# One attention and feed-forward kernel on one core: three written-out orders replaced, and the state's last products cut from 16 to 12 steps

## The chip, the cores and the metric

The kernel runs on one core of a Trainium2 chip. Its time is the device time of one execution in microseconds. The profile shows one execution; its span starts with the first instruction and ends with the last.

## The reference

`x` has the shape 8 x 8 x 512 x 64 (batch, head, row, depth) and `state` 8 x 8 x 32 x 64. All inputs and the output are float32.

```python
scores = scale * x @ state.T            # 512 x 32 for each batch and head
a = softmax(scores);   xread = a @ state
scores2 = scale * state @ x.T           # 32 x 512
a2 = softmax(scores2); sread = a2 @ x
y = concat([xread, sread], axis=rows)   # 544 rows for each batch, 8 heads x 64 = 512 columns
xn = (y - mean) / sqrt(var + 1e-6) * g_ln
out = y + relu(xn @ w_ch1) @ w_ch2      # 512 -> 2048 -> 512
```

Each softmax subtracts the row's maximum and divides by the sum plus 1e-9. The output is 8 x 544 x 512.

## The kernel before, in words

Every float32 factor of a large product is scaled by a power of two and split into two float16 parts, a high one (`hi`) and what is left (`lo`). A product of two split factors is taken in three float16 terms (`TERMS`: hi hi, hi lo, lo hi). The TensorE (PE) does the products; the ScalarE (ACT) writes high parts and exponentials, the VectorE (DVE) low parts, reductions and small arithmetic, the GpSimd (POOL) a few element-wise steps; the SyncE (SP) issues nearly all transfers.

The 512 rows of a batch go through the first layer in a shortened way. Since `xread = a @ state`, `state_products(b)` multiplies the state by the first weights once (a `matrix` for each of four units u of 512 hidden columns), and `first_products(b)` multiplies the softmax numerators (`ea`) by it. `hidden` applies the relu and splits the result; `second_products(b)` multiplies by the second weights. For batch 0, `second_products_by_units` does this unit by unit as the weights become ready. `attention(b)` does the rest of a batch: loads (`x_f`, `s_j`, `s_r`), scaling, transposes by DMA (`sT`, `xT`, `ebT`), scores, both softmaxes, the read of the state (`read_state`, L396, then `fold_halves`, L409, and `sread`), copies of the numerators (`ek`), and the product `mix` (L432), which gives the rows to be normalised and added at the end. The 256 rows of the state's reads of all batches are kept in DRAM (`sread_rows`) and go through both layers at the very end: `state_rows`, `state_hidden` (L657) and `second_products(B)`.

The weights arrive as 64-bit words of which two 32-bit halves are put together. `weights1(u)` loads them (`raw`), rebuilds float32 numbers in `words` (`w1_t`), takes out the column means (L516), finds the largest column sum (L525) for the scale, splits, and copies four pieces of 256 KB into `w1c[u]`, in which the high and low parts of a head lie on different partition halves. `weights2(u)` does the like for the second weights.

Each of these functions is a generator that yields its instructions one at a time. `issue` gets a list of such streams and a written-out order: letter a is the first stream, b the second, and the number is the place within the stream. Each engine carries out its own instructions in this order; an instruction that waits holds back all behind it on its engine. Transfers issued by SP are in SP's order in the same way. At the seam of two orders an engine's first steps of the second can stand before last steps of the first: the trace shows loads and a reduction of the next batch there.

There are three orders. PLAN is the prologue: a `gain`, b `attention(0)`, c to f `weights1(0..3)`, g `state_products(0)`, h `first_products(0)`, i to l `weights2(0..3)`, m `attention(1)`, n `state_products(1)`, o `second_products_by_units`, p `common_scale`, q `first_products(1)`, r `second_products(1)`, s `attention(2)`, t `state_products(2)`. BATCH is used four times (b = 2 to 5): a `first_products(b)`, b `second_products(b)`, c `attention(b+1)`, d `state_products(b+1)`. LAST holds batches 6 and 7 and the state's rows.

Places that matter below, by number:

- in `weights1` (c, d, e, f): 0 and 1 load; 2 to 7 rebuild words; 8 the means on PE; 9 to 12 their subtraction on DVE; 13 sizes on ACT; 14 their sum on PE (L525); 15 to 18 the scale on DVE; 19 the high half on ACT; 20 the low half on DVE; 21 and 22 copies of the high half, 23 and 24 of the low half. The copies read `raws[1]`, and `weights2` writes its `w2_t` into buffers that served so: that of i is the one from which c21 to c24 read, that of j the one from which f21 to f24 read;
- in `attention` (b, m, s, or c in BATCH): 0 and 1 load `x_f`; 2 `s_j`; 3 to 6 `s_r`; 11 the reduction over `s_j` on DVE; 23, 28, 33 the transposes of `sT` and `xT`; 34 and 35 the split of `s_r`; 36 and 37 the scores; 38 to 40, 49 to 55 and 60 the first softmax; 41 to 45 the second softmax with the transpose `ebT` (45); 56 `read_state`; 57, 58 the fold; 59 `sread`; 63 to 71 the copies to `ek`; 72 to 75 the stores of `sread`; 77 and 79 the two halves of `mix`. For batch 0 the numbers differ: 14, 15, 18, 20 and 32 are low parts and reductions on DVE, 40 is `ebT`, 58 and 59 `read_state` and the copy after it;
- in `state_products` (g, d in BATCH): 0, 3, ..., 21 the products, two for a unit.

In the PSUM, `accumulator` gives five buffers in turn and `banks` one pair, used by the scores, the read of the state and both halves of `mix` one after the other. `rows`, `quad` and `halves` are pairs of buffers, used in turn.

Of the kernel before, what the change touches and what calls it, by code (L numbers as in the profile page):

```python
# [9 lines left out]
F16 = mybir.dt.float16  # L10
# [16 lines left out]
SN = 4.0  # L27
# [37 lines left out]
BATCH = (  # L65
# [7 lines left out]
LAST = (  # L73
# [698 lines left out]
```

## Time and profile before

| | before |
|---|---|
| median of 3 runs | 707.6 us (705.15 to 709.07) |
| the profiled execution | 707.91 us |
| its span | 706.1 us |
| mean granted clock of PE | 0.974 |
| PE busy | 655.7 us (93%) |
| DVE busy | 370.9 us (53%) |
| ACT busy | 365.3 us (52%) |
| POOL busy | 68.0 us (10%) |

Where the profile gives slices, each is a fortieth of the span and each digit the busy tenths. Nearly all instructions carry L110, the line of the helper that records them, so they are told apart by the names of what they write and read ("out<-in"). In a list in order of time, the columns are start (us), duration (us; of the whole group where "x" is over 1), engine, line, operation, shape, count, and in brackets how long the engine had been idle before and what ended it. SPq is SP's queue of transfers: its durations are those of issuing, not of landing. The chain is the sequence of work that ended last, followed back to the start.

### The profile page before, as it was taken

To read this page: it belongs to the slowest core of one execution; us is meant where nothing else is said; L and a number is where in the kernel's file an instruction comes from. 1 tells how busy PE (TensorE), PEld (TensorE's weight loads), DVE (VectorE), ACT (ScalarE), POOL (GpSimd) and SP (SyncE) were. 2 spreads that over 40 slices of the span, in tenths; PEclk is the share of its full clock that TensorE was granted. 3 is DMA by queue.
4 is the path that set the end of the run, shared out by engine and by line. 5 is a ranking of instruction groups with operands and counts; after the bars stand their busy time and mean duration, and the time that the engine had idled before them with its cause. 6 is when DMAs were issued, how large, how long until landed. Compare 5 with 4: busy or idle time off the path is not lost.

```text
span 706.1 us, 10278 instructions
## 1 busy us (share of the span) xinstructions
PE 655.7 (93%) x4129; PEld 320.8 (45%) x4132; DVE 370.9 (53%) x670; ACT 365.3 (52%) x588; POOL 68.0 (10%) x54
## 2 busy tenths in 40 slices
PE   1565989999999999899999999999999999999997
PEld 0232645444453444444444444444444345445763
DVE  5995889655624454354635462545365834421120
ACT  5585889986413933295419541773287545410220
POOL 0000463211200002000200020002000200000000
PEclk9867899999999999999999999999999999999999
DMA  8988794636251032503070306130524060140001
GB/s 325 326 217 197 232 209 119 123 74 135 59 138 61 8 60 55 148 30 68 16 185 32 68 8 162 63 64 8 124 90 68 1 135 5 59 61 1 31 31 30
DMA packets 97392, 67.52 MB, mean 96 GB/s; under 512 B 73600, under 2 KB 89472, under 8 KB 96896
## 3 DMA queue, kind: packets, MB, share of 16 engines
q1 hardware_dynamic: 95424, 63.19, 35.1%
q0 software_dynamic: 864, 3.15, 2.5%
q8 instruction: 32, 0.52, 0.3%
q10 hardware_dynamic: 1056, 0.53, 0.3%
q14 instruction: 16, 0.13, 0.1%
HBM read 28.05 MB, written 9.44 MB: 53 GB/s over the span
## 4 chain that ended last, share of the span: by engine, by line
PE 70%; DVE 9%; DMA 8%; SPq 5%; ACT 4%; POOL 2%; issue 1%; POOLq 0%; DVEq 0%; ACTq 0%
PE acc L673 37%; PE acc L616 20%; SPq L110 5%; PE acc L657 4%; PE acc L582 3%; DMA w1c<-raw 2%; POOL ts L110 2%; DVE w_t L110 2%; PE acc L516 2%; DMA s_j<-in_state_dram 1%; DMA s_r<-in_state_dram 1%; PE banks L432 1%; DMA raw<-in_moe_w_ch_dram 1%; DVE raw L110 1%; DMA ebT<-eb 1%
## 5 line engine op out<-in xcount | busy, mean ns | idle before, releaser
L673 PE MATMUL acc<-w2h,hid 128*128 128x512 f16 x1632 | 368.2, 382 | 0.0
L673 PEld LDWEIGHTS <-hid 128*128 128x128 f16 x1632 | 158.2, 99 | 192.7 <-issue 12.6
L616 PE MATMUL acc<-ea,matrix 128*128 128x512 f16 (+1 forms) x864 | 176.1, 356 | 1.0 <-DVE matrix L110 0.7
L616 PEld LDWEIGHTS <-matrix 128*128 128x128 f16 x864 | 82.6, 98 | 84.6 <-issue 5.5
L110 DVE TENSOR_TENSOR hid<-strip,hid 128x512 f16<-128x512 f32 x120 | 81.2, 697 | 71.4 <-ACT hid L110 71.1
L110 ACT ACTIVATE strip<-acc,hs 128x512 f32<-128x512 f32 x112 | 75.5, 681 | 53.5 <-PE acc L616 29.6
L110 ACT ACTIVATE hid<-strip 128x512 f16<-128x512 f32 x136 | 83.0, 626 | 7.6 <-PE acc L673 4.9
L110 ACT ACTIVATE matrix<-acc 128x512 f16<-128x512 f32 x64 | 36.2, 602 | 64.1 <-PE acc L582 64.1
L110 DVE SCALAR_TENSOR_TENSOR xr<-acc,of_second,xr 128x512 f32<-128x512 f32 x28 | 21.0, 748 | 64.7 <-PE acc L673 64.6
L110 DVE SCALAR_TENSOR_TENSOR matrix<-acc,matrix 128x512 f16<-128x512 f32 x64 | 41.8, 680 | 20.8 <-ACT matrix L110 20.7
L582 PE MATMUL acc<-w1c,sT 128*32 128x512 f16 x512 | 38.2, 397 | 10.7 <-DMA w1c<-raw 10.3
L110 POOL TENSOR_TENSOR ts<-ts,mA 128x1024 f32<-128x1024 f32 (+1 forms) x8 | 16.1, 2016 | 232.8 <-DVE mA L110 202.6
L110 ACT ACTIVATE strip<-acc,hr 128x512 f32<-128x512 f32 x8 | 5.4, 686 | 49.4 <-PE acc L657 49.4
L110 POOL TENSOR_TENSOR rs<-rs,mhalf 128x4 f32<-128x4 f32 (+1 forms) x10 | 9.5, 955 | 199.6 <-DVE rs L110 199.6
L657 PE MATMUL acc<-xsT,w1c 128*128 128x256 f16 x256 | 28.4, 273 | 0.0
L110 POOL TENSOR_TENSOR hid<-strip,hid 128x512 f16<-128x512 f32 x16 | 22.1, 1405 | 58.7 <-ACT hid L110 58.6
L110 DVE SCALAR_TENSOR_TENSOR x<-x_f,x_s,x 128x512 f16<-128x512 f32 x32 | 25.3, 804 | 4.4 <-ACT x L110 4.3
L657 PEld LDWEIGHTS <-w1c 128*128 128x128 f16 x256 | 25.1, 98 | 3.5
L110 ACT ACTIVATE xr<-banks,ux 128x1024 f32<-128x1024 f32 x14 | 15.7, 1119 | 20.2 <-PE banks L432 20.2
L110 ACT ACTIVATE ea<-ef 128x1024 f16<-128x1024 f32 (+1 forms) x9 | 8.5, 958 | 33.5 <-DVE ef L110 33.5
L110 DVE BATCH_NORM_STATS2 s<-xr 128x6 f32<-128x512 f32 x32 | 21.4, 686 | 8.1 <-ACT xr L110 7.5
L582 PEld LDWEIGHTS <-sT 128*32 128x32 f16 x512 | 10.4, 97 | 30.5 <-issue 24.0
(112 smaller groups left out, 514.4 us busy)
## 6 DMA issues: line engine op xcount, KB each, us to landing
raw<-in_moe_w_ch_dram SPq DMA_DIRECT2D x16, 1024.0 KB, 8.2
out_dram<-xr SPq DMA_DIRECT2D x16, 512.0 KB, 2.7
x_f<-in_x_dram SPq DMA_DIRECT2D x15, 512.0 KB, 5.9
w1c<-raw SPq DMA_DIRECT2D x16, 256.0 KB, 6.9
ek<-ea SPq DMA_DIRECT2D x56, 64.0 KB, 2.1
ek<-ek SPq DMA_DIRECT2D x7, 512.0 KB, 4.4
xr<-part POOLq DMA_DIRECT2D x6, 512.0 KB, 5.3
s_r<-in_state_dram SPq DMA_DIRECT2D x28, 64.0 KB, 4.1
```

The costliest lines, as they stand in the source:

```text
L110: return lambda: f(*map(now, args), **{k: now(v) for k, v in kw.items()})
L432: nc.tensor.matmul(px[:, c, D * h:D * h + D], lhsT=ek[:, h // 4, h % 4, (2 * t + c) * P:(2 * t + c + 1) * P], rhs=sk[:, h], start=True, st ...
L516: nc.tensor.matmul(ps, lhsT=gm[:, k:k + 1].broadcast_to([P, P]), rhs=t4[:, k], start=k == 0, stop=k == 3)
L582: nc.tensor.matmul(ps[32 * j:32 * j + 32], lhsT=sT[:, g, a, 32 * j:32 * j + 32], rhs=w[:, 2 * g + j // 2, j % 2], start=a == 0, stop=a == ...
L616: nc.tensor.matmul(o, lhsT=m[:, g, i, P * q:P * q + P], rhs=ea[:, s, k, g], start=g == 0 and n == 0 and (b > 0 or q % 2 == 0), stop=g == 1 ...
L657: nc.tensor.matmul(ps[:, 256 * f:256 * f + 256].rearrange("p (t n) -> p t n", t=2), lhsT=w[:, k // 2, k % 2, P * (q + f):P * (q + f) + P], ...
L673: nc.tensor.matmul(po, lhsT=hid[:, i, q, c * P:(c + 1) * P], rhs=w[:, j, q], start=first and q == 0 and n == 0, stop=last and q == 3 and n ...
```

## The change

The three orders PLAN, BATCH and LAST are replaced by others. In PLAN the streams are the same; the copies of weight halves, the loads and the steps that depend on them stand elsewhere. In BATCH the load of `s_j` (c2) comes first, two loads of `s_r` come after the transpose of `sT`, and `ebT` (c45) stands ahead of the copies to `ek`. LAST gets a further stream, `high_halves`: eight copies that bring the high halves of `w1c` together, two heads on the 128 partitions, in buffers that held raw weights before. With them `state_hidden` no longer doubles the low parts of the state's rows: it has 8 steps for high parts against `w1c` and 4 for low parts against the high halves alone, where it had 8 and 8; one product, low by low, is left out. The last eight stores go out from SP and ACT in turn.

The code:

```diff
+    high = [None] * U
+
+    def high_halves():
+
+        for t in range(2):
+            pair = extra(t, "high").bitcast(F16).rearrange("p (u k f) -> p u k f", u=2, k=4)
+            for u in (2 * t, 2 * t + 1):
+                high[u] = pair[:, u % 2]
+                for s in range(2):
+                    half = slice(64 * s, 64 * s + 64)
+                    yield do(nc.sync.dma_start, out=high[u][half], in_=w1c[u][half, :, s])
...
-            v = xn.rearrange("p (h d) -> p h d", h=H).unsqueeze(2).broadcast_to([P, H, 2, D])
-            pc = halves("pc").rearrange("p (a h i d) -> p a h i d", a=2, h=H, i=2)
-            yield do(nc.scalar.activation, pc[:, 0], v, AF.Copy, scale=SN)
-            for i in range(2):
-                yield do(nc.vector.scalar_tensor_tensor, pc[:, 1, :, i], xn.rearrange("p (h d) -> p h d", h=H), SN,
-                         pc[:, 0, :, i], ALU.mult, ALU.subtract)
...
+            v = xn.rearrange("p (h d) -> p h d", h=H)
+            pc = halves("pc")[:, 0:12 * P]
+            hi = pc[:, 0:8 * P].rearrange("p (h i d) -> p h i d", h=H, i=2)
+            lo = pc[:, 8 * P:12 * P].rearrange("p (h d) -> p h d", h=H)
+            yield do(nc.scalar.activation, hi, v.unsqueeze(2).broadcast_to([P, H, 2, D]), AF.Copy, scale=SN)
+            yield do(nc.vector.scalar_tensor_tensor, lo, v, SN, hi[:, :, 0], ALU.mult, ALU.subtract)
+            yield do(nc.sync.dma_start_transpose, out=xsT[:, t], in_=pc)
...
-        def multiply(ps, q, w, xsT):
+        def multiply(ps, q, w, wn, xsT):
             for f in range(2):
-                for k in range(H):
-                    for a in range(2):
...
+                fs = slice(P * (q + f), P * (q + f) + P)
+                for k in range(12):
+                    nc.tensor.matmul(ps[:, 256 * f:256 * f + 256].rearrange("p (t n) -> p t n", t=2),
+                                     lhsT=w[:, k // 2, k % 2, fs] if k < H else wn[:, k - H, fs], rhs=xsT[:, :, k],
+                                     start=f == 0 and k == 0, stop=k == 11, skip_group_check=True)
...
     def store_state(t):
         for j in range(4):
-            yield do(nc.sync.dma_start, out=out[4 * t + j, S:S + NS, :], in_=results[B][0][1][t][32 * j:32 * j + 32, 0])
+            yield do((nc.sync, nc.scalar)[j % 2].dma_start, out=out[4 * t + j, S:S + NS, :],
+                     in_=results[B][0][1][t][32 * j:32 * j + 32, 0])
```

The orders, cut to the lines spoken of here:

```diff
 PLAN = (
-    "b1 b3-4 b2 b0 b5 a0 b6-11 b22 b72 b12 d0 d3 b23-25 b13 b15 b14 b17-18 d2 d4 d1 d6 b19-20 d5 d7 e1 e5-6 e0 "
...
-    "m9 b59 b74 c19 c21 e20 f8 e23-24 m8 b92 m7 m10 b80 b60 c20 c22-23 i5 g6-7 f11 b90-91 m12-13 f12 g9 b93 "
-    "g10 c24 f9 m14-15 f10 f13 i3 e21 g0 g15 g1 m16 b41 m17 g11 m18 m20 f14 m31 g8 m29 g3 m24 i4 f15 i6 g4 f16 "
...
+    "b3 b0 d0 b1 b4 b2 b5-6 a0 b7-11 b22 b12 b72 b24 b13 b19 b17 d3 b23 d2 b25 b14 b20 b18 d1 d5-6 d4 d7 e1 "
...
+    "c12 c9 e18 c13 e19 m1 b39-40 d20 d23-24 b75-76 b73 e21 b92 e22 b93 c14-15 b58 f6 c16-17 f3 m6 b79 c18 i1 "
+    "b91 f4 f7 c19-20 c24 e20 c23 b77 b94 b59 m7 m11 f8 b80 f12 c21 b95 c22 f11 b74 e23-24 g6 j2 m9 m8 m10 m12 "
+    "b88 g9-10 f9 b89 f10 m13-15 g7-8 m16 i5 m17 g11 m18 f13-14 i3 i6 k0 m29 f15 g0 m24 f16 m20 i4 f17 j1 g3 "
...
 BATCH = (
-    "c3 c1 a0-1 c6 a8 a2 c2 c11 a9-10 c9 a11 a4-6 a40 c0 c8 c7 c10 a20 a32 a21-22 a7 a16-18 a3 a12-13 c12-14 "
...
-    "a47 d2 a39 a49 b13 a56 c28 a57 c33 c37 c36 c38 b6 b19 a50 c39 a51 b14 c40-41 b2 c49-50 a60 b7 b3 b8 "
-    "c42-43 a55 c44 c51-55 c60-61 a61 c65 c62 a62 b0 c63 a58 c46-47 d3 a63 a59 b15 c45 c56 c66 b16 c57 b9 c58 "
...
+    "c2 c11 c0 a8-10 a0-5 a16 a32 c8 c1 c7 c10 c9 c12 c5 a12-13 a20 a11 a44 a6-7 c13-14 a21-23 a17 a14 a33 a15 "
...
+    "a56-57 c33 c37 c36 c39 c34-35 b19 b6 c40 a54 c38 c49-50 c42 c41 c43-44 a60 b2 b14 c51-52 a55 c53 b7 a58 "
+    "c45 c56 c54-55 c60-61 a51 c66 c64 b3 a61 b8 b0 c62 c68 c76 c67 a59 a62-63 b15 b4 c57 d6-7 b20 b16 b5 d8 "
+    "b21 d3 c70 d4 c46 d5 c47-48 c58-59 d0-1 b9-10 c69 d2 d12-14 c63 c65 c71 c77-78 d21 c81 d15 d22 b22 d9-10 "
...
 LAST = (
...
+    "c5 c0 a4-6 c1 c3 a0-3 a7-8 a16 a9 a36 a12 a20 g1 c7-8 c2 g2 g7 g6 g0 c11 c10 g5 c9 c12 c4 a10-11 a13 a24 "
...
-           second_products(B - 1), state_rows(), second_products(B)], LAST)
+           second_products(B - 1), high_halves(), state_rows(), second_products(B)], LAST)
```

More of the change, by code (lines that the diff above doesn't have):

```diff
@@ L634, in first_products @@
                                           nc.gpsimd)
+    high = [None] * U
[7 more added lines that the diff above has]
+                    yield do(nc.sync.dma_start, out=high[u][half], in_=w1c[u][half, :, s])
     def state_hidden():
         xr = results[B][0][1]
-        xsT = rows("xsT").bitcast(F16).rearrange("p (t a h n) -> p t a h n", t=2, a=2, h=H)
+        xsT = rows("xsT").bitcast(F16)[:, 0:24 * P].rearrange("p (t k n) -> p t k n", t=2, k=12)
         mv, rs = yield from moments([xr[t][:, 0] for t in range(2)])
@@ L643, in state_hidden @@
             yield do(nc.vector.tensor_scalar, xn, xr[t][:, 0], mv[:, t, 0:1], rs[:, t:t + 1], ALU.subtract, ALU.mult)
-            v = xn.rearrange("p (h d) -> p h d", h=H).unsqueeze(2).broadcast_to([P, H, 2, D])
-            pc = halves("pc").rearrange("p (a h i d) -> p a h i d", a=2, h=H, i=2)
-            yield do(nc.scalar.activation, pc[:, 0], v, AF.Copy, scale=SN)
-            for i in range(2):
-                yield do(nc.vector.scalar_tensor_tensor, pc[:, 1, :, i], xn.rearrange("p (h d) -> p h d", h=H), SN,
-                         pc[:, 0, :, i], ALU.mult, ALU.subtract)
-            yield do(nc.sync.dma_start_transpose, out=xsT[:, t].rearrange("p a h n -> p (a h) n"),
-                     in_=pc.rearrange("p a h i d -> p (a h i d)"))
-        def multiply(ps, q, w, xsT):
-            for f in range(2):
-                for k in range(H):
-                    for a in range(2):
-                        nc.tensor.matmul(ps[:, 256 * f:256 * f + 256].rearrange("p (t n) -> p t n", t=2),
-                                         lhsT=w[:, k // 2, k % 2, P * (q + f):P * (q + f) + P], rhs=xsT[:, :, a, k],
-                                         start=f == 0 and k == 0 and a == 0, stop=k == H - 1 and a == 1,
-                                         skip_group_check=True)
+            v = xn.rearrange("p (h d) -> p h d", h=H)
[6 more added lines that the diff above has]
+        def multiply(ps, q, w, wn, xsT):
+            for f in range(2):
+                fs = slice(P * (q + f), P * (q + f) + P)
[3 more added lines that the diff above has]
+                                     start=f == 0 and k == 0, stop=k == 11, skip_group_check=True)
         for u in range(U):
@@ L665, in state_hidden @@
                 ps = accumulator()
-                yield do(multiply, ps, q, w1c[u], xsT)
+                yield do(multiply, ps, q, w1c[u], high[u], xsT)
                 yield from hidden(ps, hr[:, u:u + 1], h[:, 0, q:q + 2, 0:256], h[:, 1, q:q + 2, 0:256], 2)
```

73 rows, old and new, of tables (BATCH, LAST, PLAN) are left out of this document.

## The prediction

> **What bounds the kernel now.** First the page: busy time of each engine, and the 40 slices of the span (17.7 us each).
>
> ```profile
> PE 655.7 (93%) x4129; PEld 320.8 (45%) x4132; DVE 370.9 (53%) x670; ACT 365.3 (52%) x588; POOL 68.0 (10%) x54
> PE   1565989999999999899999999999999999999997
> DVE  5995889655624454354635462545365834421120
> PEclk9867899999999999999999999999999999999999
> ```
>
> PE is full from the eighth slice on, and half empty in the first four. So two kinds of gain are possible: less PE work anywhere after slice 7, or an earlier end of the prologue, where DVE (5 to 9 tenths) carries the weight preparation. A table by stage makes this exact; the columns are length, then busy us of PE, PEld, DVE, ACT, POOL, then the granted clock.
>
> ```profile
> 0.00:62.00 62.00, 33.26 (x232) 17.18 (x234) 51.02 (x90) 38.50 (x53) 2.80 (x8) 0.86 0.92 279
> 62.00:124.00 62.00, 50.56 (x416) 29.97 (x416) 50.89 (x87) 50.98 (x77) 25.36 (x18) 0.92 0.78 185
> ...
> 227.50:301.30 73.80, 71.85 (x439) 32.62 (x440) 33.60 (x58) 36.28 (x63) 4.15 (x2) 0.98 0.29 71
> 301.30:373.20 71.90, 71.27 (x448) 32.65 (x445) 37.12 (x69) 37.54 (x65) 5.16 (x3) 1.00 0.30 74
> 373.20:447.70 74.50, 72.81 (x444) 33.00 (x444) 36.89 (x69) 37.46 (x65) 5.16 (x3) 0.98 0.29 71
> 447.70:518.80 71.10, 71.10 (x448) 32.60 (x445) 36.76 (x68) 37.53 (x65) 5.16 (x3) 1.00 0.29 71
> ...
> 611.30:680.70 69.40, 69.40 (x449) 43.87 (x448) 14.32 (x25) 13.30 (x20) 0.70 (x1) 1.00 0.18 41
> ```
>
> The four middle rows are the four passes of BATCH: the same work takes 73.8, 71.9, 74.5 and 71.1 us, so the last is the undisturbed length. The state's products run in the last row, with no idle PE.
>
> **Part 1: the state's product, 12 steps instead of 16.** The chain of work that ended last, the queue of SP in order of time, and the page's DMA issues give its prices.
>
> ```profile
> 316.19 2.59 PE acc L673 x12
> 318.78 1.29 PE acc L616 x6
> ...
> 651.04 13.97 PE acc L657 x128
> ...
> 79.18 3.94 SPq L110 DMA_DIRECT2D w1c<-raw  x4
> ...
> 517.04 0.55 SPq L110 DMA_DIRECT2D sread_rows<-sread  x1
> 535.76 1.22 SPq L110 DMA_TRANSPOSE sT<-sh  x1
> ...
> w1c<-raw SPq DMA_DIRECT2D x16, 256.0 KB, 6.9
> ```
>
> `multiply` falls from 2 x 16 to 2 x 12 matmuls in each of 8 accumulations: 256 become 192. In the chain one takes 13.97 / 128 = 0.109 us, and they stand on the path, so 64 x 0.109 = 7.0 us go. Two DVE instructions and a quarter of each transpose go too; they are ahead of the product with PE covered by batch 7, and count nothing. Added are eight copies of 256 KB on SP. The nearest row is the same-sized `w1c` copy: four of them occupied SP for 3.94 us (the row at 79.18), so eight take 7.9 us of SP, and landed after 6.9 us in the median. Queued behind them on SP are `s_j` and the transposes for batch 7. SP was idle from 517.6 to 535.8, ahead of the first of these transposes, 18 us, which covers 7.9. The product itself comes, summing the new order's PE steps (1.3 us a first product, 2.6 a second), over 110 us into that stage. Cost 0; without that cover it would be at most 7.9. Taken: -7.0 (ends -7.0 and +0.9).
>
> **Part 2: BATCH, four passes.** Why are passes 1 and 3 longer? DVE's and PE's instructions in order of time, and the chain:
>
> ```profile
> 285.09 0.54 SPq L110 DMA_DIRECT2D x_f<-in_x_dram  x1
> ...
> 287.72 0.47 SPq L110 DMA_DIRECT2D s_j<-in_state_dram  x1
> ...
> 292.70 0.29 DVE L110 TENSOR_REDUCE x_am<-s_j 128x1 f32<-128x128 f32 x1 [4.38 <-DMA s_j<-in_state_dram]
> 292.97 0.29 DVE L110 TENSOR_TENSOR sread<-banks,rB 128x128 f32<-128x128 f32 x1
> ...
> 293.32 0.77 PE L432 MATMUL banks<-sk,ek 128*128 128x64 f16 x16 [1.95 <-DMA s_r<-in_state_dram]
> ...
> 294.08 4.28 PE acc L673 x12
> ...
> 440.52 4.28 PE acc L673 x12
> ```
>
> The list names `s_r` as the releaser of PE, but `mix` also needs the banks, which `sread` (c59) frees, and DVE held `sread` back: ahead of it in DVE's order stands c11 of the *next* pass, which waits 4.38 us for `s_j`. SP issued `s_j` at 287.72, as the fourth of the old pass's seven loads (c3 c1 c6 c2). PE lost 1.95 us, and the twelve matmuls behind it took 4.28 instead of the 2.59 us of the row at 316.19, a part of them at half clock. Passes 1 and 3 both show that pair.
>
> The new order has `s_j` (c2) as first load, two of the four `s_r` behind `sT`'s transpose, and 3.7 us of PE work (d0 b9 d12) between the fold and `mix` instead of 3.1 (b20 d15). `s_j` needs only its one buffer, free since early in the pass. Issued ahead of the `x_f` pair (first at 285.09) it goes 2.6 us sooner, which is over the 1.95 missing. If all passes become 71.1, the gain is 2.7 + 0.8 + 3.4 = 6.9 us. If the wait stays it is 0. I take -6.9, since pass 4 shows the same PE work without the wait.
>
> Here a rule speaks against the full sum. The Trainium skill (TensorE: Matmul & The Clock Gate, Part 1) has the array fall to half rate after an idle window of about 3.4 us; a gap of 1.95 would not do it, the slow twelve would have another cause and stay, and the sum would be 6.9 - 2 x 1.7. The rows stand against it: both slow groups follow the wait directly, and pass 4, without one, has clock 1.00.
>
> **Part 3: PLAN, the prologue.** The chain, the stages in tens, and the engines in order of time:
>
> ```profile
> 62.83 7.09 DMA w1c<-raw
> 82.23 9.02 DMA w1c<-raw
> ...
> 60.00:70.00 10.00, 2.12 (x28) 0.92 (x28) 4.66 (x14) 4.67 (x6) 0.00 (x0) 0.76 1.07 206
> ...
> 57.14 2.35 DVE L110 SCALAR_TENSOR_TENSOR raw<-w_t,of_weights,raw 128x2048 f16<-128x2048 f32 x1 [2.20 <-ACT raw L110]
> 64.58 1.96 ACT L110 ACTIVATE raw<-w_t 128x2048 bf16<-128x2048 f32 x1
> 68.77 0.58 PE L582 MATMUL acc<-w1c,sT 128*32 128x512 f16 x1 [6.62 <-DMA w1c<-raw]
> 69.94 1.23 DVE L110 SCALAR_TENSOR_TENSOR w_t<-raw 128x1024 uint32<-128x1024 uint32 x1 [3.81 <-DMA w1c<-raw]
> 71.79 0.61 PE L525 MATMUL acc<-raw,ones 128*128 128x512 bf16 x1
> 73.71 0.69 DVE L110 TENSOR_REDUCE of_weights<-acc 128x1 f32<-128x512 f32 x1 [2.55 <-PE acc L525]
> 90.53 0.38 PE L582 MATMUL acc<-w1c,sT 128*32 128x512 f16 x1 [2.70 <-DMA w1c<-raw]
> ```
>
> The copies of w1c are what the prologue waits for: from 62.8 to 69.9 PE, DVE and ACT all sit idle half the time. Read by step: unit 0's low half (c20) starts at 57.14 after 2.20 us of wait; its last copy (c24) lands at 69.9. Behind it stand g0 on PE (68.77), i4 on DVE (69.94: its `w2_t` is the buffer the copies read), and f14 on PE, because f14 comes after g0 and g15 though its input was ready at 64.58 + 1.96 = 66.5. From f14 hang f15, f19, f20, unit 3's copies (issued 79.18 to 83.1) and g21 (90.53).
>
> The new order moves c20 ahead of e20 and c19 ahead of b59 on ACT; issues c24 c23 c21 c22 before e23 e24, with e21 e22 long before; and puts f14 ahead of g0 and f15 ahead of i4. So f14 starts near 66.5 instead of 71.8: 5.3 us. On DVE, 2.20 + 3.81 + 2.55 = 8.6 us of waits lose their cause. What is late next: i7 gates k1, which stands ahead of f22 on SP; and j7, which overwrites the buffer that unit 3's copies read, comes earlier in DVE's order than those copies: with issue 5 us sooner and the 9.02 us of the old row they land near 86.5, and DVE, by its summed steps, reaches j7 near 83.8. That new wait is 2.7, so DVE nets 5.9. Early on, b14 and b20 ahead of d4, and e10 behind b32, cost about a microsecond. I take 5.3 - 0.8 = 4.5, nearest to the f14 row. Ends: the full 8.6, and a loss of 3, as much as the new j7 wait would cost if nothing else moved. From 124 on PE is full, so an earlier prologue comes through whole.
>
> **Part 4: the last stores.** SP's queue and DVE in order of time, and the instructions on `xs`:
>
> ```profile
> 699.62 4.32 SPq L110 DMA_DIRECT2D out_dram<-xs  x8
> 701.44 0.75 DVE L110 SCALAR_TENSOR_TENSOR xs<-acc,of_second,xs 128x512 f32<-128x512 f32 x1 [1.84 <-PE acc L673]
> ...
> L110 SPq DMA_DIRECT2D out_dram<-xs x8: 315/422/433, 699.6 to 703.5; - x8
> ```
>
> After the last DVE result (702.2) SP issues four stores one behind the other to 703.9. With two on each queue and ACT idle by then, two issues of 0.42 go: -0.8, if ACT's issue costs what SP's does (ends -0.8 and 0). The Trainium skill (DMA: Bandwidth & Descriptors, Issuing engines are not separate DMA queues) allows no more than the issue time either.
>
> The remaining moves in LAST find PE without slack before and after, and on POOL only neighbours change places (h11 before h3, s50 before m90): 0 for both.
>
> **Sum.** 707.9 (the profiled execution: span 706.1 and 1.8 around it; 0.3 over the median of 707.6) - 7.0 - 6.9 - 4.5 - 0.8 = 688.7; 689 said.
>
> **Rivals.**
> 1. *The wait in BATCH stays or only moves.* c11 is still the first DVE step of a pass, and runs before the old pass's end. For it: SP's loads wait for buffers, which the new list does not change. Against: `s_j` is ahead of them now. Then 689 + 6.9 = 696.
> 2. *The prologue gives nothing.* DVE is at 50.9 of 62 us in both halves, so there is little room, and the earlier copies meet more loads. Then 689 + 4.5 = 693.5; with the loss of 3, 696.5.
> 3. *The slow twelve stay without the wait* (what the page's rule would make of it): 689 + 3.4 = 692.5.
> 4. *Slower: read_state waits for its transpose.*
>
> ```profile
> 334.97 1.01 PE banks L320 x16
> ...
> 351.38 2.04 SPq L110 DMA_TRANSPOSE ebT<-eb  x1
> ```
>
> Before, `ebT` was issued 15.4 us after the scores' end; c56 came 22.6 us of PE work after them (8 x 2.6 and 1.9). Now c56 comes after 14.3 (5 x 2.6 and 1.3), though c45 is ahead of the `ek` copies. By DVE and ACT steps c45 can go out after some 6.5 us, and land by 11 to 13. If a load put ahead on SP holds it to 15.4 as before, landing near 20, each of four passes waits 5.7 us and pays 1.7 for the half clock: 689 + 4 x 7.4 = 718.6. It turns the sign from a wait of about 3 us a pass (4 x 4.7 = 18.8). That the change does not do what it says concerns only part 4, 0.8.
>
> **How the numbers follow.** Forecast (688.7, all four parts) 0.62; rival 1 0.14; rival 2 0.12; rival 3 0.07; rival 4 0.05. The range reaches down to the prologue's 8.6 (707.9 - 23.3 = 684.6) and up past rivals 1 and 2 (696.5), with the runs' own spread (705.15 to 709.07) of 1.5 more: 684 to 698. Two runs differ by about half a per cent, so 0.5% (3.5 us) is what a measurement can tell. All cases but the fourth are faster by more than that; of the fourth, a short wait gives "same". Faster 0.93, same 0.03, slower 0.04.
>
> **What would show it.** Right: 192 matmuls at L657 at 0.109 us; all four passes near 71.1, clock 1.00, no wait of DVE `x_am` on `s_j` ahead of `sread`; f14 (L525, fourth group) before the first wait of L582 on w1c, starting near 66; the first product of unit 3 near 86; two stores on each queue at the end. Wrong: a PE wait at L396 on `ebT`, a wait of `mix`, or PE's first full slice not earlier than before.

## The result, and the profile after

The changed kernel took 687.2 us in the median (686.9 to 689.6) against 706.4 for the one before on the same chip: ratio 0.973 [0.969, 0.977]. The forecast was 689. The profiled execution is 689.6 us long, its span 687.8 against 706.1, so 18.3 us are to be found in the two traces. One execution of plan_only (716.2 us, at a lower mean clock than its others) is left out of the times below as slow.

The page of the changed kernel, engine totals and slices as they were shown for before:

```profile
PE 646.6 (94%) x4068; PEld 314.3 (46%) x4068; DVE 373.7 (54%) x668; ACT 362.4 (53%) x588; POOL 67.5 (10%) x54
...
PE   1667899999999999999999999999999999999997
...
DVE  5988999656634447264536544654366834521020
...
PEclk9866999999999999999999999999999999999999
```

PE is full from the sixth slice on, before from the seventh (the prediction read the eighth). 61 matmuls fewer are recorded (64 were taken out; some records are missing from any trace). So a part of the 18.3 us seems to lie in the first slices, the rest beyond. One row divides the two: the first long group of BATCH's first products on PE, 43 matmuls of L616 that wait 0.66 us for DVE. It is called the first product of BATCH below. Here it is in order of time with the scores (L320) that follow, before and then after:

```profile
227.48 9.45 PE L616 MATMUL acc<-ea,matrix 128*128 128x512 f16 x43 [0.66 <-DVE matrix L110]
260.05 1.05 PE L320 MATMUL banks<-xT,sT 128*32 128x512 f16 x16
```

```profile
225.47 9.45 PE L616 MATMUL acc<-ea,matrix 128*128 128x512 f16 x43 [0.66 <-DVE matrix L110]
257.39 1.05 PE L320 MATMUL banks<-xT,sT 128*32 128x512 f16 x16
```

The row stands 2.0 us earlier, so the prologue gave that in this trace; from there to the end the kernel before took 706.1 - 227.48 = 478.6 us, the changed one 687.8 - 225.47 = 462.3. So 16.3 of the 18.3 us lie in BATCH and LAST.

**BATCH.** By stage, the changed kernel; the rows are length, busy us of PE, PEld, DVE, ACT, POOL, granted clock, DMA share, GB/s. The last three run from scores to scores:

```profile
0.00:62.00 62.00, 33.04 (x195) 16.07 (x195) 48.45 (x84) 38.54 (x52) 2.79 (x8) 0.81 0.92 284
62.00:124.00 62.00, 55.00 (x467) 32.87 (x467) 58.12 (x101) 53.73 (x81) 26.01 (x19) 0.97 0.80 188
...
257.39:328.50 71.11, 71.11 (x444) 32.57 (x443) 37.23 (x68) 36.87 (x64) 4.83 (x3) 1.00 0.31 75
328.50:399.61 71.11, 71.11 (x444) 32.58 (x443) 37.33 (x68) 36.87 (x64) 4.84 (x3) 1.00 0.31 75
399.61:470.72 71.11, 71.11 (x444) 32.64 (x443) 37.03 (x67) 36.87 (x64) 4.83 (x3) 1.00 0.31 74
```

PE is busy in every microsecond of these three stretches, at a granted clock of 1.00. The `mix` that waited 1.95 us for its banks now stands so, in PE's order of time:

```profile
289.39 2.76 PE L683 MATMUL acc<-w2h,hid 128*128 128x512 f16 x12
...
292.63 0.64 PE L432 MATMUL banks<-sk,ek 128*128 128x64 f16 x16
```

No wait stands in its row. The twelve matmuls of the second product (L673 before, L683 now) stand ahead of `mix` in the new order, and at 2.76 us they are not slow; behind it stand products of the state.

**LAST.** The state's products in the chain that ended last (the line that was L657 is L668):

```profile
621.27 2.62 PE acc L668 x24
623.89 2.59 PE acc L683 x12
626.48 5.24 PE acc L668 x48
...
655.15 2.62 PE acc L668 x24
```

2.62 / 24 = 0.109 us each, as before, and 192 of them. (The groups by line give 28.4 us busy for the 256 before and 16.6 + 9.6 = 26.2 for the 192 after. That is no contradiction: a single matmul is recorded with 273 ns and overlaps the next one, so two groups that alternate count the overlap twice. The chain is the row to go by.) The tail, by order of time:

```profile
681.89 3.37 SPq L110 DMA_DIRECT2D out_dram<-xs  x4
681.90 3.44 ACTq L110 DMA_DIRECT2D out_dram<-xs  x4
683.71 0.75 DVE L110 SCALAR_TENSOR_TENSOR xs<-acc,of_second,xs 128x512 f32<-128x512 f32 x1 [1.84 <-PE acc L683]
```

From the start of the last DVE instruction to the end are 687.8 - 683.7 = 4.1 us, before 706.1 - 701.4 = 4.7.

**The prologue.** PE's rows after (f8 is L516, f14 L525, unit 3's first product the L582 at 87.17), and the two stages behind them in both kernels, before first:

```profile
55.97 6.22 PE L516 MATMUL acc<-w_t,gm 128*128 128x512 f32 x8
...
68.07 1.86 PE L525 MATMUL acc<-raw,ones 128*128 128x512 bf16 x4 [2.44 <-ACT raw L110]
...
87.17 0.39 PE L582 MATMUL acc<-w1c,sT 128*32 128x512 f16 x1
```

```profile
72.00:88.00 16.00, 15.61 (x130) 11.62 (x129) 14.29 (x20) 14.40 (x23) 6.85 (x5) 0.89 0.85 251
88.00:100.00 12.00, 8.87 (x95) 5.60 (x96) 10.04 (x19) 9.07 (x16) 6.95 (x5) 1.00 1.06 207
```

```profile
72.00:88.00 16.00, 13.66 (x128) 10.98 (x127) 16.00 (x28) 14.57 (x23) 7.50 (x5) 1.00 1.06 271
88.00:100.00 12.00, 11.04 (x109) 6.74 (x103) 12.00 (x16) 10.03 (x19) 8.88 (x6) 1.00 1.01 238
```

f14 starts 3.7 us earlier (before 71.79), unit 3's product 3.4 (90.53), BATCH's first product 2.0. PE no longer waits 6.6 us for the copies of `w1c`, but from 72 to 100 us DVE is busy without a gap (16.00 of 16, 12.00 of 12), where before it had 1.7 and 2.0 us to spare. No DVE step from 60 to 130 us waits for `w1c`.

### The profile page after: what moved, and what is told of

It is laid out like the page before. It is cut to its first block, busy times and chain, and to the rows that moved or that the text cites. A ratio compares the mean times of both kernels' runs of the same rounds, so it can differ in the third digit from the quotient of the medians.

```text
span 687.8 us, 10177 instructions
## 1 busy us (share of the span) xinstructions
PE 646.6 (94%) x4068; PEld 314.3 (46%) x4068; DVE 373.7 (54%) x668; ACT 362.4 (53%) x588; POOL 67.5 (10%) x54
## 4 chain that ended last, share of the span: by engine, by line
PE 84%; DVE 7%; DMA 3%; ACT 3%; issue 1%; SPq 1%; ACTq 0%; DVEq 0%
PE acc L683 48%; PE acc L616 22%; PE acc L582 4%; PE acc L668 3%; PE acc L516 3%; DVE w_t L110 2%; PE banks L396 1%; PE banks L432 1%; PE banks L320 1%; DVE matrix L110 1%; ACT raw L110 1%; PE banks L409 1%; DMA x_f<-in_x_dram 1%; DMA ek<-ek 1%; DVE x L110 1%
## 5 line engine op out<-in xcount | busy, mean ns | idle before, releaser
L683 PE MATMUL acc<-w2h,hid 128*128 128x512 f16 x1632 | 363.4, 379 | 0.0
L683 PEld LDWEIGHTS <-hid 128*128 128x128 f16 x1632 | 157.1, 98 | 192.5 <-issue 9.3
L616 PE MATMUL acc<-ea,matrix 128*128 128x512 f16 (+1 forms) x864 | 175.2, 356 | 0.9 <-DVE matrix L110 0.7
L616 PEld LDWEIGHTS <-matrix 128*128 128x128 f16 x864 | 82.6, 98 | 82.8 <-ACT matrix L110 2.9
L110 ACT ACTIVATE matrix<-acc 128x512 f16<-128x512 f32 x64 | 35.7, 599 | 91.6 <-PE acc L582 91.6
L110 POOL TENSOR_TENSOR ts<-ts,mA 128x1024 f32<-128x1024 f32 (+1 forms) x8 | 14.4, 1802 | 230.6 <-DVE mA L110 230.6
L582 PE MATMUL acc<-w1c,sT 128*32 128x512 f16 x512 | 36.2, 389 | 0.3 <-DMA w1c<-raw 0.3
L516 PE MATMUL acc<-w_t,gm 128*128 128x512 f32 x32 | 21.0, 823 | 6.3 <-DVE w_t L110 6.3
L110 ACT ACTIVATE x<-x_f,x_s 128x512 f16<-128x512 f32 x32 | 21.4, 713 | 7.9 <-DVE x_s L110 7.9
L110 DVE TENSOR_REDUCE mB<-banks 128x2 f32<-128x1024 f32 x7 | 8.5, 1217 | 27.9 <-PE banks L320 27.9
```

What stands on the lines that cost most here:

```text
L110: return lambda: f(*map(now, args), **{k: now(v) for k, v in kw.items()})
L516: nc.tensor.matmul(ps, lhsT=gm[:, k:k + 1].broadcast_to([P, P]), rhs=t4[:, k], start=k == 0, stop=k == 3)
L582: nc.tensor.matmul(ps[32 * j:32 * j + 32], lhsT=sT[:, g, a, 32 * j:32 * j + 32], rhs=w[:, 2 * g + j // 2, j % 2], start=a == 0, stop=a == ...
L616: nc.tensor.matmul(o, lhsT=m[:, g, i, P * q:P * q + P], rhs=ea[:, s, k, g], start=g == 0 and n == 0 and (b > 0 or q % 2 == 0), stop=g == 1 ...
L683: nc.tensor.matmul(po, lhsT=hid[:, i, q, c * P:(c + 1) * P], rhs=w[:, j, q], start=first and q == 0 and n == 0, stop=last and q == 3 and n ...
```

## The experiments

The row of BATCH's first product serves as a ruler in all kernels: "first product" is its start in the profiled execution, "rest" the span less that. PLAN, BATCH and LAST say which order a kernel has; "s_j first" is the old BATCH with its c2 moved to the front; new LAST goes with the new code. Three sets of kernels were compared, each with the kernel before on the same chip.

| kernel | PLAN | BATCH | LAST | median us (lowest to highest) | ratio to before | first product | rest |
|---|---|---|---|---|---|---|---|
| before (first set) | old | old | old | 707.2 (704.1 to 711.6) | 1 | 227.5 | 478.6 |
| plan_only | new | old | old | 709.5 (704.2 to 714.5) | 1.003 [1.000, 1.006] | 228.1 | 477.4 |
| batch_only | old | new | old | 703.9 (702.2 to 704.2) | 0.9945 [0.9926, 0.9965] | 229.7 | 470.8 |
| last_only | old | old | new | 697.8 (695.8 to 699.1) | 0.986 [0.984, 0.988] | 226.7 | 469.3 |
| sj_first | old | s_j first | old | 699.3 (698.2 to 700.2) | 0.988 [0.986, 0.990] | 227.4 | 470.4 |
| c11_late | old | c11 later | old | 700.6 (700.0 to 702.0) | 0.991 [0.988, 0.993] | 229.8 | 470.5 |
| plan_sj | new | s_j first | old | 699.1 (695.1 to 701.9) | 0.988 [0.985, 0.991] | 223.0 | 470.3 |
| f14_sj | old, f14 first | s_j first | old | 696.9 (696.5 to 698.2) | 0.986 [0.983, 0.988] | 224.4 | 470.4 |
| combo | new | s_j first | new | 691.4 (687.9 to 694.3) | 0.977 [0.974, 0.980] | 230.6 | 461.9 |
| old_plan_sj | old | s_j first | new | 691.5 (690.2 to 693.9) | 0.977 [0.974, 0.979] | 227.4 | 462.0 |
| old_plan | old | new | new | 693.8 (692.9 to 699.2) | 0.982 [0.978, 0.985] | 228.8 | 462.3 |
| f14_best | old, f14 first | s_j first | new | 689.0 (688.3 to 690.0) | 0.973 [0.971, 0.975] | 225.0 | 461.9 |
| after_again | new | new | new | 690.2 (687.8 to 690.3) | 0.973 [0.971, 0.975] | 223.7 | 462.3 |

The first product and rest of before are from the profile shown ahead. Times of different sets are best compared by their ratios, since the sets ran on different chips. The last column takes only five values, to 0.6 us: 478.6 (the old BATCH and LAST), 470.3 to 470.8 (BATCH without its waits), 469.3 (the new LAST alone), 461.9 to 462.3 (both), and 477.4 for plan_only. The changed kernel was traced twice: 462.3 behind the first product both times, and first products at 225.5 and 223.7. So, as far as these traces go, the kernel repeats itself behind that row, and what scatters from one execution to the next lies ahead of it.

### Each order alone

plan_only is the kernel before with this edit:

```diff
-PLAN = ("b1 b3-4 b2 b0 b5 a0 b6-11 ...
+PLAN = ("b3 b0 d0 b1 b4 b2 b5-6 a0 b7-11 ...
```

> The kernel before with only the new PLAN. In the profile of the changed kernel, the first pass of BATCH began 2.0 us sooner than before, though f14 started 3.7 us sooner and unit 3's first product 3.4 us sooner. Theory A: the new prologue is worth 3.4 to 4.5 us, and that profile caught a costly phase of the half clock (the means of unit 3 took 6.15 us instead of 4.5). Then the ratio is 0.994 to 0.995 (about 703). Rival B: it is worth 2.0 us, the rest being lost between 90 and 125 us where DVE is full: ratio 0.997. The passes of BATCH keep their 71 to 74.6 us and their two slow groups.

It gained nothing: 1.003 [1.000, 1.006], so neither number was met. One cause is at the seam from PLAN to BATCH. DVE, then PE, in order of time:

```profile
203.95 0.28 DVE L110 TENSOR_REDUCE x_am<-s_j 128x1 f32<-128x128 f32 x1 [4.56 <-DMA s_j<-in_state_dram]
204.23 0.29 DVE L110 TENSOR_TENSOR sread<-banks,rB 128x128 f32<-128x128 f32 x1
```

```profile
204.57 0.89 PE L432 MATMUL banks<-sk,ek 128*128 128x64 f16 x16 [2.93 <-DVE sread L110]
205.30 4.44 PE L673 MATMUL acc<-w2h,hid 128*128 128x512 f16 x12
```

This is the same stall as in BATCH's passes, now also ahead of the first: c11 of the old BATCH stands ahead of PLAN's last `sread` on DVE and waits for `s_j`. The old PLAN ran into the same wait (`x_am` until 207.01, after 11.18 us), but had 24 matmuls between the fold and `mix`, where the new one has 12, and its `mix` did not wait. So the new prologue reached the fold 3.8 us earlier (197.95 against 201.75) and lost 2.93 us and a slow group (4.44 instead of 2.75) where the old BATCH received it. The wait isn't the whole reason: plan_sj, below, has no such wait, and its median gains nothing from the new PLAN either.

batch_only:

```diff
-BATCH = ("c3 c1 a0-1 c6 a8 a2 c2 c11 a9-10 ...
+BATCH = ("c2 c11 c0 a8-10 a0-5 a16 a32 c8 c1 ...
```

> The kernel before with only the new BATCH. Theory: two waits of DVE for s_j ahead of sread go, with the half clock behind them: between the first matmuls of two passes 71.1 us four times, the total 7.9 us less than before (ratio 0.989). Rival (the page's rule; the half clock is not the wait's): only 1.95 + 0.6 + 1.7 = 4.3 us less (ratio 0.994), with slow groups of 4.28 us still there.

The rest is 470.8 us, so BATCH's waits are gone, 7.8 us less. But the first product came at 229.7, and 3.3 us were gained in the median instead of 7.9. The ratio is the one that the rival named, but the trace has the theory's mechanism: no slow group is left in the passes, and the loss lies ahead of them. One cause is again at the seam. PE, in order of time:

```profile
209.71 0.91 PE L432 MATMUL banks<-sk,ek 128*128 128x64 f16 x16 [1.28 <-DMA ek<-ek]
```

With this pair of orders SP issues both `x_f` loads ahead of the copy `ek<-ek` for which `mix` waits (from 199.17, the copy at 200.57); before, one of them and an `s_r` stood there, and the copy went out at 200.02. Of the 2.2 us by which the first product is late 0.5 were lost ahead of the seam already (PE reached the fold in front of this `mix` at 202.25 instead of 201.75). The granted clock is 1.00 from 205 us to the first product, so no half clock adds to the loss at the seam.

last_only (the changed code with the old PLAN and BATCH):

```diff
+PLAN = ("b1 b3-4 b2 b0 b5 a0 b6-11 ...      (old)
+BATCH = ("c3 c1 a0-1 c6 a8 a2 c2 c11 ...    (old)
```

> The kernel before with only the new LAST and the code (the 12-step product of the state, eight copies, stores on two queues). Theory: 64 matmuls of 0.109 us make 7.0, the stores 0.6, small waits in LAST 0.9: 8.5 us less (ratio 0.988). Rival: the eight copies meet the seam of the old BATCH, where SP's loads stand, and bring a wait of DVE on s_j with its half clock there: 3.6 of it is lost (ratio 0.993).

0.986 [0.984, 0.988]; the rest is 9.3 us shorter. Part of that belongs to BATCH: its waits were somewhat shorter in this execution (469.3 - 462.0 = 7.3 us of them were left where 478.6 - 470.4 = 8.2 were before). With BATCH's waits out of the way in both, the new LAST is worth 470.4 - 461.9 = 8.5 us (f14_sj against f14_best).

### What in BATCH counts: the place of `s_j`

sj_first is the kernel before with one step moved:

```diff
-    "c3 c1 a0-1 c6 a8 a2 c2 c11 a9-10 c9 ...
+    "c2 c3 c1 a0-1 c6 a8 a2 c11 a9-10 c9 ...
```

> The kernel before with one step of BATCH moved: the load of s_j (c2) comes first in a pass instead of fourth. Theory: the wait of DVE on s_j ahead of sread was all that held mix back; the slow groups of 4.28 us and the wait of 1.95 us disappear and the total falls by 7.9 us (ratio 0.989), as with the whole new BATCH. Rival: the longer PE work ahead of mix, the two later loads of s_r or the earlier ebT do it; then this move alone leaves the passes at 76, 71.8, 74.6 and 71.0 us (ratio 1.000).

0.988 [0.986, 0.990], and a rest of 470.4: this one move brings all of BATCH's gain. The theory's number was met, and the rival's moves (more PE work ahead of `mix`, the later `s_r`, the earlier `ebT`) aren't needed for it. c11_late leaves the load where it was, and moves the waiting instruction instead:

```diff
-    "c3 c1 a0-1 c6 a8 a2 c2 c11 a9-10 c9 ... a3 a12-13 c12-14 "
+    "c3 c1 a0-1 c6 a8 a2 c2 a9-10 c9 ... a3 a12-13 c11 c12-14 "
```

> The kernel before with one step of BATCH moved: c11 (DVE's x_am, the first that needs s_j) from the fourth place of the pass's DVE work to just ahead of c12. The load of s_j stays where it was, fourth of the seven. Theory (an in-order DVE stood at x_am for s_j, and sread behind it held back mix): the wait of mix goes without an earlier load, passes of 71.1 us, ratio 0.989, 699 us as with the load first. Rival (the late load itself, or what follows x_am in its pass, is the cause): the wait stays or moves to the next pass's scores, 0.996 to 1.0, 704 to 707 us.

0.991 [0.988, 0.993], rest 470.5, so the passes gain as much as with the load first; its first product comes 2.3 us later than before's, which isn't traced. DVE in order of time, at the place where x_am and then `sread` stood before (292.70 and 292.97), then the `mix` behind it on PE:

```profile
290.40 0.22 DVE L110 TENSOR_SCALAR rB<-rB,x_i 128x2 f32<-128x2 f32 x1
290.71 0.29 DVE L110 TENSOR_TENSOR sread<-banks,rB 128x128 f32<-128x128 f32 x1
```

```profile
293.60 0.64 PE L432 MATMUL banks<-sk,ek 128*128 128x64 f16 x16
```

`sread` follows its own input, and no `mix` of the passes waits. So the load was never too late for the work that needs it; it was late for the place of its first reader in DVE's order. The releaser that the list named for PE's wait, `s_r`, was no cause: neither order puts it earlier.

### What in PLAN counts

plan_sj is plan_only with s_j first; f14_sj keeps the old PLAN but for two steps:

```diff
-    "... f10 f13 i3 e21 g0 g15 g1 ... m20 f14 m31 g8 m29 g3 m24 i4 f15 i6 ...
+    "... f10 f13 f14 i3 e21 g0 g15 g1 ... m20 m31 g8 m29 g3 m24 f15 i4 i6 ...
```

> The kernel before with the new PLAN, and with c2 (the load of s_j) moved to the front of BATCH; LAST is the old one. With c2 first alone the ratio was 0.9884 (699.25 us). Theory (the new PLAN is worth the 2.0 us by which the first BATCH product comes earlier in the changed kernel, and lost it at the seam only because s_j was issued late): no wait of mix on sread at the seam, ratio 0.9856, 697.2 us. The prediction's step (4.5 us from f14): 0.982, 694.7 us. Rival (the new PLAN gives nothing, and the 2.0 us belong to something else): 0.9884 to 0.991, 699 to 701 us.

> The kernel before with c2 first in BATCH, and in PLAN only two steps moved: f14 ahead of g0 and g15 on PE, f15 ahead of i4 on DVE. No copy of w1c is moved. The prediction's step says that f14 then starts near 66.5 instead of 71.8 us, and unit 3's first product (g21) some 5 us earlier, and that most of it comes through: ratio 0.981 to 0.983, 694 to 695 us. Theory now (DVE, full from 72 to 100 us in the changed kernel, takes over as the bound, and PE waits for its results): f14 near 66.5, but the first BATCH product only 1 to 2 us earlier: 0.986, 697.2 us. Rival (nothing: w1c's copies are what counts): 0.9884, 699.2 us.

plan_sj: the wait at the seam is gone, and in the profiled execution the first product comes at 223.0, 4.5 us before sj_first's. But that execution is the fastest of those timed; the median is 699.1, no better than sj_first (699.3), and its times reach to 701.9, so the rival's number was met. f14_sj: 696.9, with all of its times within 1.7 us, the number of "theory now". That is 2.4 us better than sj_first by the medians, though in another set, and the intervals of the two ratios overlap. The same two steps beside each other in one set bear it out: f14_best 688.3 to 690.0, old_plan_sj 690.2 to 693.9. PE, then DVE and SP in order of time:

```profile
65.62 0.59 PE L525 MATMUL acc<-raw,ones 128*128 128x512 bf16 x1 [3.71 <-ACT raw L110]
...
87.37 0.38 PE L582 MATMUL acc<-w1c,sT 128*32 128x512 f16 x1 [1.27 <-DMA w1c<-raw]
```

```profile
67.53 0.69 DVE L110 TENSOR_REDUCE of_weights<-acc 128x1 f32<-128x512 f32 x1 [2.37 <-PE acc L525]
69.46 1.23 DVE L110 SCALAR_TENSOR_TENSOR w_t<-raw 128x1024 uint32<-128x1024 uint32 x1 [1.24 <-DMA w1c<-raw]
...
73.90 0.69 DVE L110 SCALAR_TENSOR_TENSOR matrix<-acc,matrix 128x512 f16<-128x512 f32 x1 [1.90 <-ACT matrix L110]
...
77.49 2.35 DVE L110 SCALAR_TENSOR_TENSOR raw<-w_t,of_weights,raw 128x2048 f16<-128x2048 f32 x1
```

```profile
77.45 3.94 SPq L110 DMA_DIRECT2D w1c<-raw  x4
```

f14 starts where the prediction said (65.6; 66.5 in the text), 6.2 us earlier than before, and unit 3's copies still go out only 1.7 us earlier (77.45 against 79.18). Between the two, DVE takes f15 and then i4, which waits for the copies of `w1c` until 69.46 as it did before (69.94), and then waits 1.90 us for ACT's `matrix`, whose input waits for the same copies. DVE's waits in this stretch were 7.9 us before (1.53 for `matrix` at 64.78, then the 3.81 and 2.55 that the prediction shows), and 6.4 of them are still there (0.90 for `matrix` at 63.81, then 2.37, 1.24, 1.90). The copies landed sooner after their issue than before, so unit 3's first product (87.37) comes 3.2 us earlier, and BATCH's first product 3.1: half of what f14 gained, and more than the 1 to 2 us of "theory now".

### The parts put together again

combo is the changed kernel with "s_j first" for BATCH; old_plan_sj has the old PLAN too; old_plan is the changed kernel with the old PLAN; f14_best is old_plan_sj with f14_sj's PLAN; after_again is the changed kernel.

```diff
 combo:        BATCH = ("c2 c3 c1 a0-1 c6 a8 a2 c11 a9-10 ...
 old_plan_sj:  the same, and PLAN = ("b1 b3-4 b2 b0 b5 a0 b6-11 ...
 old_plan:     BATCH = ("c2 c11 c0 a8-10 ...  and PLAN = ("b1 b3-4 b2 b0 ...
 f14_best:     as old_plan_sj, with "... f10 f13 f14 i3 e21 ..." and "... m24 f15 i4 i6 ..."
```

> The changed kernel with its new PLAN and LAST, but BATCH is the old order with c2 alone moved to the front. The changed kernel's ratio is 0.9731 (687.2 us). Theory (of the new BATCH only the place of s_j matters): the same, 0.973, 687 us. Rival 1 (the rest of the new BATCH pays at the seams, where its first steps meet PLAN's or LAST's): 0.975 to 0.979, 688.5 to 691.5 us. Rival 2 (the rest of the new BATCH costs something): 0.970, 685 us.

> The changed kernel itself, beside the three below, to see how far its time scatters: the two earlier kernels with the new PLAN and s_j first scattered from 695.1 to 701.9 and from 687.9 to 694.3 us, and all of it lay ahead of BATCH's first scores. Theory (the new PLAN's prologue ends at different times from run to run, and the 687.2 us of the changed kernel and the 691.4 us with the old BATCH, s_j first, differ by that alone): a median of 688 to 691 us, runs from 686 to 694, ratio 0.973 to 0.978. Rival (the rest of the new BATCH is worth the 4 us): 687 us again, ratio 0.973, with runs within 3 us of each other.

> The old PLAN, the old BATCH with c2 moved to its front, and the changed kernel's LAST with its code. What the whole change would be without the new PLAN. From BATCH's first scores to the end the old LAST took 437.8 us and the new one 429.3, so 8.5 us less than the 699.25 us with c2 first alone: 690.7 us, ratio 0.9765, with runs within 3 us. If the new PLAN is worth the 2.0 us of the traces, the changed kernel beats this by that; if it is worth the prediction's 4.5 us, by 4.5; if its gain is eaten by its scatter, the two have the same median.

> As the kernel with the old PLAN, c2 first and the changed LAST, and f14 and f15 moved ahead in PLAN as in the run before (696.85 us with the old LAST): 8.5 us less, 688.3 us, ratio 0.9733, runs within 2 to 3 us of each other. Theory (the place of f14 is what is worth most in the new PLAN, the order of the copies adds only scatter): at least as fast as the changed kernel run beside it. Rival (the new PLAN's other moves pay too): 2 us or more slower than the changed kernel.

> The changed kernel with the old PLAN alone, so the new BATCH begins behind the old prologue. With the new BATCH alone the seam cost a wait of 1.28 us of mix on ek and a stretch at half clock, and the ratio was 0.9945 (703.9 us). Theory (orders are fitted at their seams: the new BATCH wants the new PLAN ahead of it): 8.5 us less than that, 695.3 us, ratio 0.9825, and slower than the same with the old BATCH and c2 first. Rival (the seam's loss was a chance of that run): 690.7 us, 0.9765.

after_again gave 0.973 [0.971, 0.975] on another chip, with 690.2 us where before took 708.7: the gain holds, and the absolute time is 3 us higher there. Its times lie within 2.5 us. combo (0.977 [0.974, 0.980]) met the number of its rival 1, not the theory's. In the traces it differs from after_again ahead of the first product only: 230.6 against 223.7, with the same PLAN in both. Whether the rest of the new BATCH helps the prologue or combo met worse executions isn't settled: the intervals overlap, and combo's fastest, 687.9, equals after_again's. old_plan, with the old PLAN ahead of the new BATCH, gave 0.982 [0.978, 0.985]: there the new PLAN is worth 3.6 us by the medians (against after_again), and the intervals are apart. Ahead of the BATCH with s_j first it is worth nothing, with the old LAST (699.1 against 699.3) as with the new one (combo 691.4, old_plan_sj 691.5, in two sets). So by the times new PLAN and new BATCH belong together, as the theory of the seams has it; but the place and the cause aren't settled, since old_plan's profiled `mix` waited only 0.22 us at the seam. (Its expectation speaks of half clock at batch_only's seam; the trace has none there.)

f14_best is as fast as the changed kernel (0.973 [0.971, 0.975], 689.0 against 690.2 beside it). So two steps in PLAN, one in BATCH and the new LAST give, within the noise, all that the three new orders give. It does not beat it by more than can be told.

## Why the prediction was right, step by step

- **State's product: -7.0.** Right: 64 matmuls of 0.109 us. The eight copies went out from 495.0 to 505.3 us and landed 7.2 us after their issue in the median; the product came at 621, so they cost nothing, as said.
- **BATCH: -6.9 said, -8.2 measured** (478.6 - 470.4). The mechanism was the right one, shown by two different edits. The size was too small because the passes were cut at round places. Measured from scores to scores the first three passes took 74.85, 71.85 and 74.59 us against 71.0 without the wait; the cut at 227.5 to 301.3 gave the first only 73.8. Rivals 1 and 3 fall: in the passes there is no wait of `mix`, and no slow group either (rival 3's sum should read 692.4). The rule of the Trainium skill that stood against the full sum is taken up below.
- **PLAN: -4.5 said, -2.0 in the trace.** This is the step that was mis-sized, at "from f14 hang f15, f19, f20, unit 3's copies". It was treated as one chain, of which nearly every microsecond at f14 comes through. f14_sj shows that of 6.2 us only 1.7 reach the issue of the copies and 3.1 BATCH's first product: DVE works in order, and i4 and `matrix` wait for `w1c` between f15 and the copies. In the changed kernel `w1c` comes earlier, and the new wait of 2.7 us at j7 did not come; but f8 runs at half clock for most of its time (6.22 us instead of 4.47), f14 starts at 68.07 and not near 66.5, and DVE has no gap left from 72 to 100. The 3.7 us at f14 are 3.4 at unit 3's product and 2.0 at BATCH's first product; where the last 1.4 went isn't traced. The size itself scatters: the second trace of the same kernel has the first product 3.7 us earlier than before's trace. By the medians the new PLAN is worth 3.6 us ahead of the new BATCH and nothing ahead of the old one, with or without the early `s_j`. So that it gains is shown for this pair of orders only.
- **Rival 2** (the prologue gives nothing) was right for plan_only, and in part for another reason than it gave: c11's wait, which the prediction had described for BATCH's passes and not looked for ahead of the first, took 2.93 us at the seam. Since plan_sj gains nothing either, the rest stays open.
- **The last stores: -0.8 said, -0.6 measured** (4.7 to 4.1). ACT's four issues (3.44 us) take about as long as SP's (3.37), as the term had assumed.
- **The remaining moves in LAST: 0 said, about -0.9 measured** (8.5 - 7.0 - 0.6). A part is idle PE: 0.42 us from 515 us to the last DVE result before, 0.04 from 497 us after. The other half isn't traced to an instruction.
- **Rival 4** did not come: no row shows PE waiting for `ebT` in the passes.

The sum: -2.0 - 8.2 - 8.5 = -18.7, and 0.4 come back because the new BATCH's rest is 462.3 and not 461.9 us: 18.3, against 19.2 forecast. The prologue gave 2.5 us less than said and the other terms together 1.6 more. So the sum came out better than its terms, and that is luck: two errors of unlike sign, and a prologue that scatters by more than either.

## What to carry to other kernels

When an in-order engine stands in a wait, look at what is queued behind it: moving the reader cures the stall as well as an earlier load, and one step may do what a whole new order does. Test a new part with the seam that it will have, since alone it may lose its gain there, as plan_only and batch_only did in part. Before summing a step that comes earlier, go down the order of each engine that its chain passes and note the next thing each waits for; and look for a row that splits the span into a part that scatters and a part that repeats.

## What the hardware showed beside that

The half clock keeps a fixed grid. In every trace here its stretches, but for the last one, near the end of the span, last 3.41 us or a multiple of it (6.83, 10.24, 13.65), and within one execution their starts are whole multiples of 3.41 us apart. Cut by that grid, PE's busy share of one stretch goes with the clock of the next. Before (passes 1 and 3, then pass 2 and what followed pass 3); then last_only (passes 2 and 3); then combo, in the prologue:

```profile
290.59:294.00 3.41, 1.46 (x27) 0.83 (x26) 1.30 (x4) 0.60 (x1) 0.00 (x0) 0.99 0.65 188
437.37:440.78 3.41, 1.72 (x27) 0.95 (x27) 1.65 (x4) 0.82 (x2) 0.00 (x0) 0.99 0.57 167
...
365.69:369.10 3.41, 2.78 (x32) 1.44 (x33) 2.21 (x5) 1.71 (x2) 0.00 (x0) 1.00 0.58 172
440.78:444.19 3.41, 3.41 (x9) 1.21 (x8) 1.46 (x3) 0.89 (x1) 0.00 (x0) 0.51 0.46 168
```

```profile
362.36:365.77 3.41, 1.59 (x27) 0.76 (x26) 1.23 (x4) 0.60 (x1) 0.00 (x0) 1.00 0.88 249
437.45:440.86 3.41, 1.64 (x28) 0.94 (x27) 1.65 (x4) 0.83 (x2) 0.00 (x0) 1.00 0.61 175
```

```profile
88.25:91.66 3.41, 1.20 (x11) 0.49 (x10) 0.73 (x1) 0.94 (x3) 1.15 (x1) 0.98 1.31 141
91.66:95.07 3.41, 3.41 (x21) 2.15 (x21) 3.15 (x8) 1.32 (x3) 0.00 (x0) 0.50 1.03 203
```

PE busy 1.46 of 3.41 us (43%) was followed by half clock, as were 1.72 (50%), 1.59 (47%) and 1.20 (35%); 2.78 (82%) was not, and nor was 1.64 (48%). So in the passes the bound lies about half. In the prologue it is blurred: in sj_first 2.66 of 3.41 us (78%, from 59.31) was followed by half clock too. The Trainium skill (TensorE: Matmul & The Clock Gate, Part 1) has a free-running window of 3413 ns, which agrees with the grid; but its table asks for an idle window, and here a window half busy was enough. So a wait of some 1.8 us is enough or not by little: in last_only those of passes 2 and 3 (1.82 and 1.77 us) leave 47% and 48% busy, and only the first was followed by half clock. A stretch of it costs about 1.7 us, the 4.28 less 2.59 of the slow group. That the same wait, split over two stretches of the grid, would cost nothing follows from this, but no run shows it.

This is also the likely cause of the prologue's scatter, though no run takes the grid away: its waits of 1 to 4 us on the copies meet the grid differently in each execution. With the same PLAN, combo fell to half clock from 91.6 to 98.4 us behind a wait of 2.21 us on `w1c` and reached the first product at 230.6; after_again and plan_sj, at clock 1.00 there, at 223.7 and 223.0. Half clock for 6.8 us can explain 3.4 of these 7 at most (an estimate: half of the work of that time is lost), so the rest has another cause, which isn't traced.
